# Attention and mixture-of-experts kernel: when the weights of the experts are fetched

## The chip, the cores and the metric

One core of one Trainium2 chip runs the whole program in a single launch. The metric is the time of the program on the device in microseconds (us), as the median of the runs shown. A profiled execution gives a trace: the start and the length of every instruction on the five engines (TensorE is PE, its weight loads PEld, VectorE is DVE, ScalarE is ACT, GpSimd is POOL, SyncE is SP) and of the packets that the 16 DMA engines move.

## The reference

Inputs are q, k and v of shape (8 batches, 8 heads, 576 positions, 64), a gate matrix (512 x 8), and for each of 8 experts w1 (512 x 1024) and w2 (1024 x 512), all float32, and a capacity of 80.

```python
scores = scale * np.matmul(q, k.transpose(0, 1, 3, 2))
mask = block_i >= block_j                  # causal in blocks of 64
attn = softmax(where(mask, scores, -1e9))
x = matmul(attn, v)                        # 4608 tokens x 512
logits = x @ w_gate; expert_idx = argmax(logits); gate_w = the winner's probability
for e in range(8):
    tok_idx = tokens of expert e, at most capacity (80), those with the largest gate_w
    h = np.maximum(x[tok_idx] @ w1[e], 0.0)
    out[tok_idx] = gate_w[tok_idx, None] * (h @ w2[e])
```

All rows of `out` that no expert takes are zero.

## The kernel before, in words

**Attention.** The work is cut into 32 pairs of heads (8 batches x 4 pairs), run in turns i of some 8 us. A table of steps (TURN) says what is issued in a turn, and for which pair: loads of Q and K (`ld`) for the pair five turns ahead, their transposes on DVE (`T`, line 639) two turns ahead, V (`vn`, `vt`) three turns ahead, then scores on PE (line 663), maxima on DVE, exponentials on ACT, transposes of the probabilities on PE (line 744), their copies out of PSUM (`PT`, line 792, on ACT or DVE), and the products with V (line 770). Each engine works through its own list in order. Q loads, half of the K loads and the stores go out on SP's queue; from pair 5 on the other half of the K loads, and V, go out on POOL's. Loads have four buffers each. After four pairs a batch's result goes to a scratch in DRAM (`xs`, line 429). In the last five turns SP also writes zeros over the output (18 x 512 KB).

**Weights.** There are 16 weight tiles of 2 MB, in the order w1[0], w2[0], w1[1], w2[1], and so on to w2[7]. Three of them (FW0) have memory of their own and are loaded during attention, in 16 pieces on POOL's queue: 4 of 512 KB for w1[0], 8 of 256 KB for w2[0], 4 of 512 KB for w1[1]. The generator `early` hands out one piece per `next`, in two of every three turns (line 914).

The other 13 tiles need memory that attention held, so they come at the end, on SP's queue, one DMA each (line 362). They have nine buffers in all, the three early ones included; from the tenth tile on a tile waits until its buffer's last user is through.

**Choice of tokens.** After the last pair the kernel finds, for each expert, the rows of x to take (`gi`), and gathers them from `xs` by indirect DMAs on POOL's queue (`xg`, `fetch`, line 1101): those of experts 0, 1 and 2 at once, later ones after the first product of the expert three before. DVE divides each by the sums of the softmax (`xn`, line 1211), PE transposes them (line 1254; for expert 0 line 1275), and each expert e makes `first(e)` with w1 (lines 1227 and 1240) and `second(e)` with w2 (line 1325, results in `av`, `ps`, and for the last expert `pm`); a scatter on POOL's queue writes the rows out.

**Order of the late tiles.** `half()` issues the first half (1 MB) of w2[1] while the tokens are still being chosen; the second half waits for `fetches[HOLD]`, HOLD = 1, that is for gather 1 to land. Then a list `behind` gives each tile what it waits for: w1[2] the second half's landing, w2[2] gather 1, and every later one of the first six the landing of the tile two before it.

The places that the change touches, in a few lines:

```python
if i >= 2 and i % 3:
    next(early, None)
...
other_half(fetches[HOLD])
behind = [loaded.ins, fetches[HOLD]]
for _ in range(FWA + FWC + FWB - 1):
    weights(1, behind.pop(0))
    behind.append(loaded.ins)
```

Of the kernel before, what the change touches and what calls it, by code (L numbers as in the profile page):

```python
# [7 lines left out]
F32 = mybir.dt.float32  # L8
# [10 lines left out]
P = 128  # L19
BLK = 64  # L20
NT = 5
FW0, FWA, FWC, FWB = 3, 3, 1, 2
# [166 lines left out]
def tile_attn_moe(ctx, tc, q, k, v, w_gate, w1, w2, capacity, out, xs=None, dbg=None):  # L189
# [3 lines left out]
    E, _, F = w1.shape  # L193
# [5 lines left out]
    KP = DM // P  # L199
# [55 lines left out]
    def clear(i, eng=nc.gpsimd):  # L255
        if ov is not None:
            if 0 <= i < nz:
                return eng.dma_start(ov[i], zero.rearrange("p (r d) -> p r d", r=2))
        elif i == 0:
            for j in range(NTOK // BLK):  # L260
                nc.sync.dma_start(out[j * BLK:(j + 1) * BLK, :], zero[0:BLK, 0:DM])
# [18 lines left out]
    after = const.tile([P, P], F32, name="after")  # L280
# [15 lines left out]
    def constants():  # L296
        nc.gpsimd.memset(dl, 1e-9)
        nc.gpsimd.memset(zero, 0.0)
        nc.gpsimd.iota(iota_e, pattern=[[1, E]], base=-E, channel_multiplier=0,
                       allow_small_or_imprecise_dtypes=True)  # L300
        nc.gpsimd.iota(iota_v, pattern=[[0, NT], [1, E]], base=-E, channel_multiplier=0,
                       allow_small_or_imprecise_dtypes=True)
        nc.gpsimd.memset(iota_v[0:BLK, 0], 64.0)
        nc.gpsimd.memset(lgT[:, 0:BLK], 0.0)
        nc.gpsimd.memset(sameR3, 0.0)
        nc.gpsimd.memset(ones, 1.0)
        nc.gpsimd.iota(iota_s, pattern=[[1, CHUNK]], base=0, channel_multiplier=0,
                       allow_small_or_imprecise_dtypes=True)
        nc.gpsimd.iota(iota_p, pattern=[[0, 1]], base=0, channel_multiplier=1, allow_small_or_imprecise_dtypes=True)
        nc.gpsimd.iota(iota_c, pattern=[[1, 16]], base=0, channel_multiplier=0,  # L310
                       allow_small_or_imprecise_dtypes=True)
# [14 lines left out]
    def constants3():  # L326

        nc.vector.tensor_tensor(iota_c16, sameR, iota_c, op=ALU.mult)
        nc.vector.tensor_reduce(iota_r, iota_c16, axis=AX.X, op=ALU.add)
        nc.vector.scalar_tensor_tensor(cap, cf[:, 1:2], 4294967296.0, cf[:, 0:1], op0=ALU.mult, op1=ALU.add)  # L330
        nc.vector.tensor_tensor(caplt, iota_p, cap, op=ALU.is_lt)

    nw, loaded = 0, None
    wpools = [wp] * FW0

    wlist = [x for e in range(E) for x in ((w1, e), (w2, e))]
    wt_ = {}
# [5 lines left out]
    def loads(n, after=None):  # L343

        nonlocal nw, loaded
        for _ in range(n):
            src, e = wlist[nw]
            w_ = wpools[nw % len(wpools)].tile([P, KP * F], F32, name="w")
            nw += 1
            wt_[src is w2, e] = w_ = w_.rearrange("p (a f) -> p a f", f=src.shape[2])  # L350
            if nw <= FW0:
                yield from (nc.gpsimd.dma_start(w_[:, a], src[e][a * P:(a + 1) * P]) for a in range(w_.shape[1]))
                continue
            piece(w_, src[e], 0, w_.shape[1], after)

    def piece(w_, src, a0, a1, after=None):

        nonlocal loaded
        with ExitStack() as order:
            if loaded is not None:  # L360
                order.enter_context(tc.issue_after(loaded.ins))
            loaded = nc.sync.dma_start(w_[:, a0:a1], src[a0 * P:a1 * P].rearrange("(a p) f -> p a f", p=P))
        if after is not None:
            tc.add_manual_dep(loaded.ins, after.name, mybir.DependencyInfo(
                mybir.DependencyClass.Sync, mybir.DependencyReason.DATA))

    def half():

        nonlocal nw
        src, e = wlist[nw]  # L370
        w_ = wpools[nw % len(wpools)].tile([P, KP * F], F32, name="w")
        nw += 1
        wt_[src is w2, e] = w_ = w_.rearrange("p (a f) -> p a f", f=src.shape[2])
        na = w_.shape[1]
        piece(w_, src[e], 0, na // 2)
        return lambda after: piece(w_, src[e], na // 2, na, after)

    Pt = [{u: pb.tile([P, 2, w], F32, name=f"P{u}_{i}") for u, w in WIDE.items()} for i in range(2)]  # L380

# [9 lines left out]
    def banks(use, where=BANKS):  # L391
        return [psp[i].tile([P, 512], F32, name=f"bank{i}") for i in where[use]]
# [401 lines left out]
    def warm(n, wt, after=None):  # L794

        if not n:
            return
        with ExitStack() as order:
            if after is not None:
                order.enter_context(tc.issue_after(after.ins))  # L800
            for i in range(n):
                last = nc.tensor.matmul(wt.rearrange("p (a c) -> p a c", c=P), lhsT=identr,
                                        rhs=identr.unsqueeze(1).broadcast_to([P, 4, P]), start=(i == 0),
                                        stop=(i == n - 1))
        return last
# [86 lines left out]
    with tc.manual_schedule():  # L892
        warm(WARM[0], banks("g")[0])
        early = loads(FW0)
        for i in range(-LEAD, n):
            held.clear()
            if i == -1:
                nc.sync.dma_start(ci, capacity.bitcast(U32).partition_broadcast(P))
                for h in range(2):
                    nc.sync.dma_start(wgd[h * D:(h + 1) * D, :, h * E:(h + 1) * E], wg_v[h])  # L900

            for _ in range(min(5, nz - kept - cleared) if i >= n - 5 else 0):
                clear(cleared, nc.sync)
                cleared += 1
            if i == 1 - LEAD:
                nc.scalar.activation(early_exp, ramp[:, 2, 0:1], AF.Exp)
                constants()
            if i == -1:
                constants2()
            if i == 5:  # L910
                nc.gpsimd.tensor_copy(cf, ci)
            if i == 7:
                constants3()
            if i >= 2 and i % 3:
                next(early, None)
            shared = i > 1 and (i < NP or i % NP == 0)
            for d, what, *args in FIRST if i == -1 else AHEAD if i == -2 else LAST if i == n - 1 else SHARED if shared else TURN:
                if what in slots_:
                    slots_[what]()
                elif 0 <= i + d < n and not (what == "flip" and n - NP <= i + d < n - 2):  # L920
                    getattr(pairs[i + d], what)(*args)
            if n - NP <= i + valued < n - 2:
                pairs[i + valued].flip()
            if i >= flipped and (i - flipped) % NP == NP - 1 and i - flipped < n - 1:
                enqueue(batches[(i - flipped) // NP])
        for _ in early:
            pass
        while not turns:
            t()
        bt = batches[B - 1]  # L930
        pairs[n - 2].flip()
        for _ in recips[0]:
            pass
        bt.store_sums()
        pairs[n - 1].take("V00", "a")
        bt.flip(NP - 1, 0, 8)
        pairs[n - 1].take("V01", "a")
        pairs[n - 1].take("V1", "v")
        att.close()
        fwa = late.enter_context(tc.tile_pool(name="fwa", bufs=FWA, **right, **tw))  # L940
        wpools += [fwa] * FWA
        bt.logits2(LAST_BANKS)
        bt.logits_by_token(NP - 1)
        bt_, mark = turns.pop(0)
        bt_.turn2(banks("av")[0])
        mark()
        for _ in bt.products(range(NP - 1)):
            pass
        bt.flip(NP - 1, 8, S // 32)
        bt.store_x()  # L950
        other_half = half()
        for _ in (*bt.products((NP - 1,)), *bt.shift()):
            pass
        bt.expo()
        nc.gpsimd.tensor_copy(seen[0:1], dl[0:1, 0, 0:1])
        found, weighed = bt.first_of(), bt.weight()
        for g_ in (found, found, found, weighed, found, weighed):
            next(g_)
        bt.turn_gated()
        bt.turn2(banks("L")[0])  # L960
        while small:
            t()
        for _ in bt.placed():
            pass
# [52 lines left out]
        for h in range(2):  # L1017
            vec.max_index(cidx[:, h], cand16[:, h], Wf[:, h * HW:(h + 1) * HW])

    HOLD = 1  # L1020
    pen = sel.tile([P, 2, NH], F32, name="pen")
    pool.tensor_scalar(pen, key, scalar1=0.0, scalar2=8192.0, op0=ALU.is_lt, op1=ALU.mult)
    pool.tensor_tensor(pen, pen, iota_c[:, 0:NH].unsqueeze(1).broadcast_to([P, 2, NH]), op=ALU.add)
# [71 lines left out]
    xg, fetches = [], []  # L1095
# [100 lines left out]
    wpools += [fwc] * FWC + [fwb] * FWB  # L1196

    assert cleared == nz or ov is None
    other_half(fetches[HOLD])
    behind = [loaded.ins, fetches[HOLD]]  # L1200
    for _ in range(FWA + FWC + FWB - 1):
        weights(1, behind.pop(0))
        behind.append(loaded.ins)

# [369 lines left out]
```

## Time and profile before

| what | value |
|---|---|
| runs | 385.63, 386.33, 386.37 us; median 386.33 |
| profiled execution | 387.1 us, of which the trace's span is 385.3 |
| mean granted TensorE clock | 0.997 of full speed |
| PE busy in the span | 367.5 us (95%) |
| ACT, DVE, POOL busy | 287.5, 286.0, 183.7 us |
| read from HBM, written to it | 63.21 MB, 20.33 MB |
| weight pieces on POOL's queue | 8 of 512 KB, 8 of 256 KB |
| late weight tiles on SP's queue | 12 of 2048 KB, 2 halves of 1024 KB |

Attention takes the time up to about 277 us, the choice of the tokens up to about 293, the eight experts the rest. Busy PE is not PE at its peak, and a share of the DMA engines above 1 means that packets of one engine overlap. Idle time of an engine that nothing waits for costs nothing; so the first question of any row is who waits behind it.

### The profile page before, as it was taken

To read this page: it belongs to the slowest core of one execution; us is meant where nothing else is said; L and a number is where in the kernel's file an instruction comes from. 1 tells how busy PE (TensorE), PEld (TensorE's weight loads), DVE (VectorE), ACT (ScalarE), POOL (GpSimd) and SP (SyncE) were. 2 spreads that over 40 slices of the span, in tenths; PEclk is the share of its full clock that TensorE was granted. 3 is DMA by queue.
4 is the path that set the end of the run, shared out by engine and by line. 5 is a ranking of instruction groups with operands and counts; after the bars stand their busy time and mean duration, and the time that the engine had idled before them with its cause. 6 is when DMAs were issued, how large, how long until landed. Compare 5 with 4: busy or idle time off the path is not lost. (4 is left out here: it accounts for less than half of the span.)

```text
span 385.3 us, 15173 instructions
## 1 busy us (share of the span) xinstructions
PE 367.5 (95%) x5973; PEld 248.4 (64%) x5973; DVE 286.0 (74%) x804; ACT 287.5 (75%) x880; POOL 183.7 (48%) x377
## 2 busy tenths in 40 slices
PE   5899899999999999999999999999999999999983
PEld 3566567666766666676676676666668555555652
DVE  5889799999999999999999999999986210101001
ACT  1799799999999999999999999999521333332221
POOL 6246376665976766786587664430132121110000
PEclk9999999999999999999999999999999999999998
DMA  9969999999999999999999999999795899999950
GB/s 125 154 120 187 133 184 173 154 231 132 164 215 151 162 202 181 155 176 196 177 174 245 145 182 191 279 393 407 157 212 167 278 384 374 384 391 398 399 211 26
DMA packets 169937, 84.43 MB, mean 219 GB/s; under 512 B 132590, under 2 KB 151886, under 8 KB 169857
## 3 DMA queue, kind: packets, MB, share of 16 engines
q1 hardware_dynamic: 158368, 61.80, 76.3%
q0 software_dynamic: 9120, 21.27, 24.2%
q8 instruction: 49, 0.80, 1.0%
q10 hardware_dynamic: 2368, 0.30, 0.6%
q14 instruction: 32, 0.25, 0.3%
HBM read 63.21 MB, written 20.33 MB: 217 GB/s over the span
## 5 line engine op out<-in xcount | busy, mean ns | idle before, releaser
L710 ACT ACTIVATE P<-bank,negm 128x512 f32<-128x512 f32 (+3 forms) x320 | 157.6, 549 | 10.6 <-DVE negm L699 5.9
L663 PE MATMUL bank<-T,qt 64*128 64x320 f32 (+3 forms) x512 | 98.8, 494 | 1.4 <-DVE PT L792 1.3
L770 PE MATMUL bank<-PT,vn 128*64 128x64 f32 (+3 forms) x1288 | 88.9, 292 | 0.0
L699 DVE TENSOR_REDUCE negm<-bank 128x1 f32<-128x320 f32 (+2 forms) x192 | 83.4, 474 | 5.6 <-PE bank L689 5.4
L792 ACT COPY PT<-bank 128x512 f32<-128x512 f32 x149 | 77.2, 636 | 3.8 <-PE bank L744 3.3
L770 PEld LDWEIGHTS bank<-PT,vn 128*64 128x64 f32 x1288 | 57.1, 137 | 26.7 <-ACT PT L792 3.4
L646 POOL TENSOR_SCALAR qt<-T 128x128 f32<-128x128 f32 (+2 forms) x96 | 31.2, 344 | 88.4 <-DVE T L639 88.4
L744 PEld LDWEIGHTS bank<-ident,P 64*128 64x128 f32 (+1 forms) x1600 | 58.0, 137 | 11.8 <-issue 6.6
L663 PEld LDWEIGHTS bank<-T,qt 64*128 64x128 f32 x512 | 47.9, 187 | 26.8 <-ACT PT L792 15.2
L744 PE MATMUL bank<-ident,P 64*128 64x64 f32 (+1 forms) x1600 | 63.5, 225 | 1.3 <-ACT P L710 0.6
L710 ACT ACTIVATION_READ_ACCUMULATOR P<-bank,negm 128x1 f32 x256 | 61.7, 241 | 0.0
L699 DVE TENSOR_REDUCE raw<-bank 128x1 f32<-128x64 f32 (+1 forms) x128 | 51.8, 444 | 2.3 <-PE bank L663 2.0
L639 DVE STREAM_TRANSPOSE T<-ld 128x576 f32<-128x576 f32 x64 | 49.1, 768 | 5.7 <-DMA ld<-in_k_dram 4.0
L632 POOL DMA_DIRECT2D vn<-in_v_dram x58 | 45.8, 792 | 1.2 <-issue 0.7
L1325 PE MATMUL av<-w,hT 128*32 128x512 f32 (+2 forms) x320 | 39.0, 553 | 0.0
L624 POOL DMA_DIRECT2D ld<-in_k_dram x54 | 37.3, 695 | 2.7 <-DMA ld<-in_q_dram 2.7
L1334 DVE SCALAR_TENSOR_TENSOR y<-av,comb,yt 80x512 f32<-80x512 f32 (+1 forms) x8 | 5.6, 696 | 43.0 <-ACT yt L1332 42.9
L1240 PE MATMUL ps<-xsT,w 128*64 128x80 f32 x896 | 33.1, 234 | 0.3 <-issue 0.3
L1240 PEld LDWEIGHTS ps<-xsT,w 128*64 128x64 f32 x896 | 31.9, 137 | 1.9 <-PE av L1325 1.0
L1340 POOL DMA_INDIRECT out_dram<-y,si x8 | 7.5, 936 | 53.6 <-DVE y L1334 41.3
L1332 ACT ACTIVATE yt<-ps,gfar 32x512 f32<-32x512 f32 (+2 forms) x18 | 11.4, 635 | 26.1 <-PE ps L1325 26.0
L792 DVE COPY PT<-bank 128x512 f32<-128x512 f32 x43 | 29.3, 683 | 0.3
(202 smaller groups left out, 423.9 us busy)
## 6 DMA issues: line engine op xcount, KB each, us to landing
w<-in_moe_w_dram SPq DMA_DIRECT2D x12, 2048.0 KB, 17.6
xs<-Y SPq DMA_DIRECT2D x32, 288.0 KB, 5.5
out_dram<-zero SPq DMA_DIRECT2D x18, 512.0 KB, 7.6
ld<-in_q_dram SPq DMA_DIRECT2D x126, 72.0 KB, 5.5
vn<-in_v_dram POOLq DMA_DIRECT2D x58, 128.0 KB, 5.1
ld<-in_k_dram SPq DMA_DIRECT2D x72, 72.0 KB, 5.3
w<-in_moe_w_dram POOLq DMA_DIRECT2D x8, 512.0 KB, 6.6
ld<-in_k_dram POOLq DMA_DIRECT2D x54, 72.0 KB, 6.4
```

Of the source, the lines that this page charges most:

```text
L624: eng.dma_start(self.nat[x][r], (q, k)[x][b, h0 + h, :, 32 * i:32 * i + 32] .rearrange("(g r) d -> r g d", r=32))
L632: eng.dma_start(self.vn[:, h], v[b, h0 + h, 0:512].rearrange("(j p) d -> p j d", p=P))
L639: nc.vector.transpose(t, self.nat[x].rearrange("p g d -> p (g d)"))
L646: nc.gpsimd.tensor_scalar(qb[:, to], tb[:, of], scalar1=SCALE, scalar2=1.0, op0=ALU.mult, op1=ALU.mult)
L663: nc.tensor.matmul(s[h][:, c:c + n], lhsT=q_[:, P * t - BLK:P * t + BLK], rhs=k_[:, 0:n], start=(c == 0 and g != "2"), stop=(g == "1"))
L699: nc.vector.tensor_reduce(to[:, b, h:h + 1], self.s[g][h][:, c:c + n], axis=AX.X, op=ALU.max, negate=True)
L710: nc.scalar.activation(Pt[self.i % 2][u][:, h, c1:c1 + n], self.s[g][h][:, c:c + n], AF.Exp, bias=self.negm[:, t, h:h + 1], scale=1.0, acc ...
L744: nc.tensor.transpose(pt[c][0:cols.stop - cols.start, n_ * BLK:(n_ + 1) * BLK], row[u][r, h, cols], ident[r, r])
L770: nc.tensor.matmul(a4[r] if c0 is None else av[r, BLK * c0:BLK * (c0 + b1 - b0)], lhsT=self.vn[:, h, j, :], rhs=self.PT[:, h, row, b0:b1]. ...
L792: (nc.scalar.copy if (eng or TAKE[x]) == "a" else nc.vector.tensor_copy)(*self.out.pop(x))
L1240: last = nc.tensor.matmul(dst(b)[64 * c:64 * (c + 1)], lhsT=w_[:, a, col:col + 64], rhs=x_[a], start=(a == 0), stop=(a == n - 1))
L1325: last = nc.tensor.matmul(to[col:col + s1 - s0, c0:c1], lhsT=hT[:, a, s0:s1], rhs=w_[:, a, c0:c1], start=(a == ends[0]), stop=(a == ends[1 ...
```

## The change

Three edits. The early pieces are handed out from turn 6 on, in place of turn 2. `half()` is gone: w2[1] is one DMA like the others. HOLD is 0, and w2[1] and w1[2] both wait for gather 0; w2[2] then waits for w2[1], w1[3] for w1[2], and so on.

```diff
-    def half():
-        nonlocal nw
-        src, e = wlist[nw]
-        w_ = wpools[nw % len(wpools)].tile([P, KP * F], F32, name="w")
-        nw += 1
-        wt_[src is w2, e] = w_ = w_.rearrange("p (a f) -> p a f", f=src.shape[2])
-        na = w_.shape[1]
-        piece(w_, src[e], 0, na // 2)
-        return lambda after: piece(w_, src[e], na // 2, na, after)
...
-            if i >= 2 and i % 3:
+            if i >= 6 and i % 3:
                 next(early, None)
...
-        other_half = half()
...
-    HOLD = 1
+    HOLD = 0
...
-    other_half(fetches[HOLD])
-    behind = [loaded.ins, fetches[HOLD]]
-    for _ in range(FWA + FWC + FWB - 1):
+    behind = [fetches[HOLD], fetches[HOLD]]
+    for _ in range(FWA + FWC + FWB):
         weights(1, behind.pop(0))
         behind.append(loaded.ins)
```

POOL's list around the start of turn 2, before the change (`w` is a weight piece, `vn` and `vt` V, `ld` K, `qt` the scaled Q):

```order
L646 TENSOR_SCALAR qt_145<-T_653 128x384
L632 DMA vn<-in_v_dram 128x4x64 x2
L634 DMA vt_146<-in_v_dram 64x2x64
L352 DMA w<-in_moe_w_dram 128x1024
L624 DMA ld_674<-in_k_dram 32x18x32 x2
L646 TENSOR_SCALAR qt_144<-T_814 128x128
```

and after it (the lines of the file are 13 lower):

```order
L633 TENSOR_SCALAR qt_145<-T_653 128x384
L619 DMA vn<-in_v_dram 128x4x64 x2
L621 DMA vt_146<-in_v_dram 64x2x64
L611 DMA ld_672<-in_k_dram 32x18x32 x2
L633 TENSOR_SCALAR qt_144<-T_812 128x128
```

The piece between `vt` and the K loads is gone there. The 16 pieces now stand at turns 7, 8, 10, 11 (w1[0]), 13, 14, 16, 17, 19, 20, 22, 23 (w2[0]) and 25, 26, 28, 29 (w1[1]); before they stood at 2, 4, 5, 7, then 8 to 19, then 20, 22, 23, 25. The last of them comes after the last V load on POOL's queue.

SP's list where the late tiles begin, before, with the semaphores that each waits for (DMAHW and DMASW are the landings of DMAs of SP's and of POOL's queue; DMASW5, 6 and 7 are gathers 0, 1 and 2):

```order
L429 DMA xs<-Y 32x18x128 [waits DMAHW7_49]
L362 DMA w<-in_moe_w_dram 128x4x512 [waits DMASW4_49,DMASW3_49,DMASW5_49,DMASW2_49,DMASW6_49,DMASW1_49,DMASW7_49,DMASW0_49,DMAHW0_49,PE_49,Activation_49]
L362 DMA w<-in_moe_w_dram 128x4x512 [waits DMAHW1_49,DMASW6_49]
L362 DMA w<-in_moe_w_dram 128x4x1024 [waits DMASW4_49,DMASW1_49,DMAHW1_49,PE_49,DMAHW2_49,Activation_49,Pool_49]
L362 DMA w<-in_moe_w_dram 128x8x512 [waits DMAHW3_49]
L362 DMA w<-in_moe_w_dram 128x4x1024 [waits DMAHW4_49,DMAHW2_49]
```

and after:

```order
L416 DMA xs<-Y 32x18x128 [waits DMAHW7_49]
L362 DMA w<-in_moe_w_dram 128x8x512 [waits DMASW4_49,DMASW3_49,DMASW5_49,DMASW2_49,DMASW6_49,DMASW1_49,DMASW7_49,DMASW0_49,DMAHW0_49,PE_49,Activation_49]
L362 DMA w<-in_moe_w_dram 128x4x1024 [waits DMASW4_49,DMASW3_49,DMASW7_49,PE_49,DMAHW1_49,Activation_49,Pool_49]
L362 DMA w<-in_moe_w_dram 128x8x512 [waits DMAHW2_49,DMAHW0_49]
L362 DMA w<-in_moe_w_dram 128x4x1024 [waits DMAHW3_49,DMAHW1_49]
```

The two half DMAs (128x4x512) are one (128x8x512). Before, the third row waited for the second half (DMAHW1) as well as for its own lane (DMAHW2); now the second row waits for no other weight, and the third for the first (DMAHW0). The waits for DMASW4, 3 and 7 in the second row are those for V loads whose memory the tile takes (before DMASW4 and 1).

DVE's list after the first gathers, before (`xn` is the division of a gather; the first row here is gather 1's, the later one gather 2's):

```order
L1211 TENSOR_TENSOR xn<-xg 80x128 x4
L1148 COPY gfar<-comb 32x8 x2
L1148 COPY gfar<-comb 16x8
L1155 CAST ids<-gi 80x8
L1161 TENSOR_SCALAR vm,nval<-cand 128x12
L1163 TENSOR_TENSOR chk<-slot,cap 128x2
L1171 MEMSET dif 128x8
L1211 TENSOR_TENSOR xn<-xg 80x128 x4
L1190 TENSOR_SCALAR comb<-ids 80x8
```

and after, from the same `dif` on:

```order
L1157 MEMSET dif 128x8
L1176 TENSOR_SCALAR comb<-ids 80x8
L1148 TENSOR_SCALAR chk<-sameE,nval 128x8
L1154 TENSOR_SCALAR good<-pm,iota_p,caplt 80x8
L1164 TENSOR_REDUCE nb<-pm 128x1
L1158 SCALAR_TENSOR_TENSOR dif<-occ,caplt,good 80x8
L1160 TENSOR_REDUCE dsum<-dif 128x1
L1162 SCALAR_TENSOR_TENSOR dsb<-cap,dsum 128x1
L1196 TENSOR_TENSOR xn<-xg 80x128 x4
```

Gather 2's division has moved behind the checks that end in `dsb`. PE's and ACT's lists are the same as before.

## Rows read from the trace of the kernel before

**Rows 1.** Waits of PE, whole span: us in total, times, longest

```profile
PE pm L1325 <- SPq L1386: 1.7, 1, 1.7
PE bank L663 <- DVE PT L792: 1.3, 1, 1.3
```

**Rows 2.** Timeline of PE, 370.5 to 374: start, length, what, idle before

```profile
373.38 0.52 PE L1325 MATMUL pm<-w,hT 128*32 128x384 f32 x3 [1.73 <-SPq L1386]
```

**Rows 3.** Timeline of SP's queue, the issues of late weight tiles

```profile
293.28 0.39 SPq L362 DMA_DIRECT2D w<-in_moe_w_dram  x1
...
299.33 0.37 SPq L362 DMA_DIRECT2D w<-in_moe_w_dram  x1
...
347.83 7.43 SPq L362 DMA_DIRECT2D w<-in_moe_w_dram  x1
```

**Rows 4.** DMA issues at 299.33 and 347.83: count, KB, us to landing

```profile
w<-in_moe_w_dram SPq DMA_DIRECT2D x1, 2048.0 KB, 8.5
...
w<-in_moe_w_dram SPq DMA_DIRECT2D x1, 2048.0 KB, 25.4
```

**Rows 5.** Stretches: engines' busy us, clock, DMA share, GB/s

```profile
298.00:300.00 2.00, 2.00 (x42) 1.25 (x42) 0.00 (x0) 0.44 (x1) 0.71 (x1) 1.00 0.06 18
...
302.00:371.00 69.00, 68.65 (x1220) 42.38 (x1214) 10.31 (x33) 22.56 (x40) 10.46 (x11) 1.00 1.03 386
```

**Rows 6.** Timeline of all engines, 28 to 46

```profile
31.95 0.59 POOL L352 DMA_DIRECT2D w<-in_moe_w_dram  x1
...
32.05 1.09 SPq L624 DMA_DIRECT2D ld<-in_k_dram  x2
...
35.82 2.40 PEld L770 LDWEIGHTS bank<-PT,vn 128*64 128x64 f32 x38 [0.54 <-DMA vn<-in_v_dram]
...
39.01 0.27 PE L776 MATMUL bank<-PT,vt 64*64 64x64 f32 x1 [0.19 <-DMA vt<-in_v_dram]
...
41.42 0.78 DVE L639 STREAM_TRANSPOSE T<-ld 128x576 f32<-128x576 f32 x1 [2.78 <-DMA ld<-in_k_dram]
...
43.36 1.99 PE L663 MATMUL bank<-T,qt 64*128 64x512 f32 x12 [1.28 <-DVE PT L792]
```

**Rows 7.** The stretch 35 to 40, columns as in rows 5

```profile
35.00:40.00 5.00, 4.81 (x64) 3.25 (x62) 3.61 (x9) 4.87 (x19) 3.17 (x7) 1.00 1.24 177
```

**Rows 8.** Waits of DVE from 30 to 260, the only one for a load

```profile
DVE T L639 <- DMA ld<-in_k_dram: 2.8, 1, 2.8
```

**Rows 9.** The pieces' line: count, ns min/median/max, first and last start

```profile
L352 POOL DMA_DIRECT2D w<-in_moe_w_dram x16: 568/574/591, 32.0 to 220.7; - x16
```

**Rows 10.** The stretch 276 to 278, columns as in rows 5

```profile
276.00:278.00 2.00, 1.74 (x55) 1.46 (x52) 1.68 (x8) 0.37 (x1) 0.33 (x2) 1.00 0.18 21
```

**Rows 11.** The last store of x (issued 280.23): KB, us to landing

```profile
xs<-Y SPq DMA_DIRECT2D x1, 288.0 KB, 5.2
```

**Rows 12.** Timeline of POOL, 288 to 301: the gathers of experts 0 to 3

```profile
288.71 1.13 POOL L1101 DMA_INDIRECT xg<-xs,gi  x1 [3.46 <-DVE gp L1115]
290.14 0.99 POOL L1101 DMA_INDIRECT xg<-xs,gi  x1 [0.30 <-issue]
291.43 0.97 POOL L1101 DMA_INDIRECT xg<-xs,gi  x1 [0.31 <-issue]
299.29 0.96 POOL L1101 DMA_INDIRECT xg<-xs,gi  x1 [6.88 <-PE ps L1240]
```

**Rows 13.** Timeline of DVE, 290.5 to 300: divisions of gathers 0 and 1

```profile
291.94 0.89 DVE L1211 TENSOR_TENSOR xn<-xg 80x128 f32<-80x128 f32 x4 [0.50 <-DMA xg<-xs,gi]
293.29 0.90 DVE L1211 TENSOR_TENSOR xn<-xg 80x128 f32<-80x128 f32 x4 [0.45 <-DMA xg<-xs,gi]
```

**Rows 14.** DMA issues at 291.43 and 299.29: us to landing

```profile
xg<-xs,gi POOLq DMA_INDIRECT x1, 3.0
...
xg<-xs,gi POOLq DMA_INDIRECT x1, 6.9
```

**Rows 15.** Timeline of PE, 293 to 305: transposes of expert 1's input

```profile
296.27 0.50 PE L1254 MATMUL pm<-ident,xn 80*128 80x80 f32 x4
```

## The prediction, made before the changed kernel was run

> **What bounds the kernel now.** Read first who TensorE (PE) waited for over the whole span [rows 1]. Apart from the 4.2 us at the start there are two waits over a microsecond: 1.7 us before `pm` of line 1325, the second product of the last expert, and 1.3 us before `bank` of line 663, a score matmul early in the attention part. PE is busy through nearly everything else, so time can be gained only at places where PE stands still, and lost where a new wait arises.
>
> The timeline puts the first wait at the very end: PE resumes at 373.38 after 1.73 idle, so it was free at 371.65 [rows 2]. The view names SyncE's line 1386 as releaser, but that branch was long done. The other candidate is a DMA: the last weight tile was issued at 347.83 and took 25.4 us, so it landed at 373.2 [rows 3, 4], 0.15 before PE moved. The last weight tile sets the end. Its stream runs at 386 GB/s with the DMA engines fully taken from 302 to 371, but from 298 to 300 they moved only 18 GB/s [rows 5]: a hole. It comes from the code: after the first half of tile w2[1] (1 MB, issued ahead of the gathers), the other half waits for the second gather (issued 293.28), and the next tile waits for that half (issued 299.33) [rows 3].
>
> The early wait is a chain. VectorE (DVE) idles 2.78 us before a transpose of K at 41.42, for the K loads; PE idles 0.19 at 39.01 for a V load and 1.28 at 43.36 for what DVE produced after that transpose. The K loads that land late were issued by SyncE at 32.05, right behind the first early weight piece, which GpSimd issued at 31.95 [rows 6].
>
> **The change part by part.**
>
> *Early pieces from turn 6.* The 16 pieces stay the same; the one at 31.95, and those of turns 4 and 5, go five turns or more later. What stood behind the piece was its 512 KB. At the 177 GB/s that all queues moved from 35 to 40 [rows 7] this is 524 KB / 177 = 2.96 us; at the 386 GB/s of [rows 5] it is 1.36 us. The K loads, which released DVE at about 41.3, land 1.36 to 2.96 earlier; DVE's 2.78 shrink by as much as there is. PE's 1.28 at 43.36 needs 1.28 of that, so it goes at both ends, and the V load's 0.19 with it: 1.28 + 0.19 = 1.47. More is possible: the PE weight load at 35.82 waited 0.54 for another V load [rows 6], part of which may go, so up to 2.0. Less is possible too, if what follows is not ready sooner; the lower end is 0. I take 1.5, at the row's own two gaps, because nothing else of PE stands in the way: its 50 transposes before 43.36 had ended 1.28 earlier. A turn saved here moves everything after it, since from 50 to 260 DVE never waits for a K or Q load again [rows 8] and PE waits for next to nothing [rows 1].
>
> On this the Trainium skill ("DMA: Bandwidth & Descriptors", section "Anatomy of one DMA — SWDGE (gpsimd) path") gives a fit of 2.0 us plus bytes / 436 GB/s; by that the piece occupies the engines 1.2 us, and as an estimate only 1.2 of the 1.28 would go, a sum of 1.4. The trace moved much less than 436 GB/s in that stretch [rows 7], so I stay with the row.
>
> What the pieces cost where they now stand: the four 512 KB pieces of w1[0] at turns 7, 8, 10 and 11 (three of these held 256 KB pieces), and two 512 KB pieces more at turns 28 and 29. The other 15 pieces of before, seven of them of 512 KB and the last at 220.7 [rows 9], are followed by no DVE wait for a load [rows 8]: their cover is the five turns that loads run ahead. Cost 0. At turns 28 and 29 the zeroing of the output already fills the DMA engines; 1 MB more is 1.05 MB / 386 = 2.7 us of backlog. The row 276 to 278 shows a share of 0.18, so 1.6 us of it vanish there [rows 10]; the remaining 1.1 would delay the last stores of x, which landed at 280.23 + 5.2 = 285.4 [rows 11]. The first gather started at 288.71, held by its indices [rows 12], 3.3 us later. Cost 0; without that cover 1.1.
>
> *No half tile, everything behind the first gather.* Three edits, one answer. Gather 0 is in use at 291.94 and gather 1 at 293.29 [rows 13], and SyncE issued its half at 293.28. So the release moves from 293.28 to about 291.93. In the changed order the first two whole tiles, w2[1] and w1[2], are both released there, and the third waits for the first of them: two are always in flight, and the hole at 298 to 300 has no cause left. The pair that before went out at 299.33 (w1[2] and w2[2]) was in the same state: two whole tiles into idle queues. From there on before and after have the same chain, with 7.40 us lead (299.33 - 291.93) and one tile more to move. One tile costs (373.2 - 307.8) / 11 = 5.95 us, from the landing of w1[2] (299.33 + 8.5) to that of the last tile [rows 3, 4], other traffic included. So the last tile lands 7.40 - 5.95 = 1.45 earlier, at 371.8. PE is free at 371.65 and resumes 0.15 after the landing: 371.95 in place of 373.38, a gain of 1.43. Bounds: at the pure rate a tile costs 2.097 MB / 386 = 5.43, the lead is 1.97 and the whole 1.73 goes; with gather 2's 166 KB (0.43 us) now inside the stream on top of 6.4 for a slow tile, the lead is 0.6. I take 1.43. What is late next is PE itself: behind the last product nothing changes.
>
> The cost of this edit is on the gathers. Gather 1 (issued 290.14) now has weights released 1.8 us behind it. Before, gather 2 (291.43) had a half tile released 1.85 us behind it and took 3.0 us to land; gather 3 at 299.29, with two tiles released at its side, took 6.9 [rows 12, 14]. Gather 1 stands as gather 2 did: about 3, as now. Gather 2 will take up to 6.9, landing at 298.3; its division in DVE moves behind the checks in the new order, and PE wants it only for the third expert's input, after 304. Cost 0.
>
> **The sum.** Profiled execution: 387.1 (span 385.3). 387.1 - 1.5 - 1.43 = 384.2. The median of the three runs is 386.33, 0.8 below it: 386.33 - 2.9 = 383.4.
>
> **The rivals.**
>
> A. *Only the tail gains.* The shift of turn 3 is swallowed later, by a DMA backlog that stands anyway (the share is above 1 from 35 to 40 [rows 7]). Against it: the quiet of DVE afterwards [rows 8]. 386.33 - 1.43 = 384.9.
>
> B. *The missing half is missed.* It is 1 MB that travelled while the engines were partly idle. If the hole stays (some other wait holds the second tile), the last tile lands 1.05 MB / 386 = 2.7 later, less 1.35 for the earlier release: 374.6, PE 1.35 later than before; with the early gain 386.33 - 1.5 + 1.35 = 386.2, no change. The Trainium skill ("Perfetto Trace Analysis", section "DMA Optimizations") speaks for this side: splitting a DMA lets part of it start sooner when the engines are idle. Before does show the half going ahead, and also the hole right behind the split tile [rows 5].
>
> C. *Gather 1 is caught behind the weights.* If it takes 6.9, it lands at 297.0; 0.9 us of divisions [rows 13] bring 297.9 against PE's transposes at 296.27 [rows 15]: PE stalls 1.7. That eats the wait at the end, no more: the tail gains nothing, 386.33 - 1.5 = 384.8.
>
> D. *The pieces cost the same wherever they stand: slower.* Each 512 KB piece at turns 7, 8, 10 and 11 brings PE the 1.47 that the one of turn 2 brought: 4 x 1.47 = 5.9 against 2.9 gained, 386.33 + 3.0 = 389.3. It decides where K loads are issued under some 9 us before DVE needs them, as at 32.05 for 41.42; from two collisions on the gain is gone. Against it: the pieces at 50 to 221 collided with nothing visible [rows 8, 9].
>
> E. *The change doesn't do what it says*: the release still waits for gather 1 through another semaphore, and turn 3 waits for loads late anyway. 386.3.
>
> **How the numbers follow.** Forecast 0.67, A 0.10, B 0.08, C 0.07, D 0.06, E 0.02. About 0.2% (0.8 us) is what a measurement of this kernel can tell from no change. Faster: forecast, A and C, 0.84. Same: B and E, rounded to 0.09. Slower: D and a piece of B without the early gain, 0.07. The forecast's own range is 386.33 - 2.0 - 1.73 = 382.6 to 386.33 - 1.3 - 0.6 = 384.4; for 8 in 10 it reaches over A and C, to 385.2, and down to 382.4.
>
> **What would show it.** In the changed profile: no DVE wait for K near 41 and no PE wait of 1.28 near 43; every event of the tail some 1.5 earlier; two whole tiles issued within a microsecond of each other just after gather 0; no stretch under 100 GB/s between the first tile and the last; PE's wait before the last `pm` under 0.5 us; gather 2 slower, gather 1 as before. Wrong would be: a DVE wait for loads at turns 8 to 12, or a PE wait before the transposes of the second expert's input.

## The result, and the profile after

Six runs of each kernel, side by side: before 386.87 us median (385.63 to 388.76), after 382.91 (382.71 to 383.15). The ratio is 0.9892, with an interval of 0.9864 to 0.992. All ratios of this document leave out runs that lie over 1.5% above the fastest of their kernel, nine of twelve in e11 and three in e3, so that those two are read by their medians. The forecast was 383.4 (382.4 to 385.2), faster: right. The profiled execution took 382.95 (span 381.2), against 387.1 (span 385.3).

The gain came out larger than worked out, 3.96 against 2.93, and one thing stands beside it that the forecast did not have: the kernel before scatters over three microseconds, the one after over half a microsecond. Most of the experiments are about this.

Waits of PE in the changed kernel, the largest after the 4.2 us at the start (us in total, times, longest). Line numbers are 13 to 15 lower than before:

```profile
PE bank L731 <- ACT P L697: 0.6, 1, 0.6
PE pm L1310 <- ACT hT L1280: 0.6, 1, 0.6
PE bank L566 <- DVE sp L555: 0.5, 1, 0.5
```

The 1.7 of the last product is 0.6, and the 1.3 of turn 3 is gone [rows 1]. Turn 2 in the timeline, without the piece that stood at 31.95 [rows 6]:

```profile
31.98 1.09 SPq L611 DMA_DIRECT2D ld<-in_k_dram  x2
...
35.51 2.75 PE L757 MATMUL bank<-PT,vn 128*64 128x320 f32 x40
38.19 0.27 PE L762 MATMUL bank<-PT,vn 64*64 64x64 f32 x1
...
39.00 0.73 DVE L626 STREAM_TRANSPOSE T<-ld 128x576 f32<-128x576 f32 x1
```

DVE transposes this K at 39.00 with no wait, where before it waited 2.78 and started at 41.42. Also, the 40 products with V take 2.75. The same row of the kernel before:

```profile
35.08 3.48 PE L770 MATMUL bank<-PT,vn 128*64 128x320 f32 x40
```

Take the start of each PE instruction before minus after, and call it the lead. It is -0.43 just before 35 us (the start differs a little from run to run), 0.80 at 39, 2.24 at 44, 2.3 from 50 to 140 and 2.7 from 150 to 298. So turns 2 and 3 gave 2.7: 1.2 up to 39, where V was late, and 1.4 from there to 44, where K was. The further 0.3 came near 145; its cause is not shown.

The gathers and the stream of weights, after. GpSimd's timeline and SyncE's queue, then the DMA issues of 288 to 292, that at 288.74 and that at 296.60 (count, KB, us to landing), then two stretches (columns as in rows 5):

```profile
286.01 1.14 POOL L1087 DMA_INDIRECT xg<-xs,gi  x1 [3.44 <-DVE gp L1101]
...
296.60 0.96 POOL L1087 DMA_INDIRECT xg<-xs,gi  x1 [6.90 <-PE ps L1225]
```

```profile
289.43 10.22 SPq L362 DMA_DIRECT2D w<-in_moe_w_dram  x3
```

```profile
w<-in_moe_w_dram SPq DMA_DIRECT2D x2, 2048.0 KB, 12.5
...
xg<-xs,gi POOLq DMA_INDIRECT x1, 4.0
...
xg<-xs,gi POOLq DMA_INDIRECT x1, 7.4
```

```profile
298.00:300.00 2.00, 2.00 (x24) 0.60 (x20) 0.00 (x0) 0.00 (x0) 0.00 (x0) 1.00 1.03 411
302.00:367.00 65.00, 65.00 (x1167) 40.21 (x1164) 10.26 (x33) 21.26 (x39) 10.54 (x11) 1.00 1.03 385
```

Where 18 GB/s moved at 298 to 300 [rows 5], 411 do. Two tiles go out at 289.43 and 290.05, right behind gather 0. The lead of 2.7 at 298 falls to 1.8 at 305, is back at 2.7 at 352, and is 4.0 from the last product to the end: the tail gave 1.3. The last product, PE and ACT:

```profile
368.87 0.44 ACT L1280 ACTIVATE hT<-ps 128x320 f32<-128x320 f32 x1 [1.78 <-PE ps L1225]
369.38 0.52 PE L1310 MATMUL pm<-w,hT 128*32 128x384 f32 x3 [0.56 <-ACT hT L1280]
```

The view puts the 0.56 down to ACT, but the last tile landed at 369.25 too, 0.13 ahead of PE. Which of the two it is stays open up to the last experiment.

### The profile page after: what moved, and what is told of

Its sections match the earlier page's. It is cut to its first block, busy times and chain, and to the rows that moved or that the text cites. A ratio compares the mean times of both kernels' runs of the same rounds, so it can differ in the third digit from the quotient of the medians.

```text
span 381.2 us, 15172 instructions
## 1 busy us (share of the span) xinstructions
PE 366.9 (96%) x5973; PEld 247.1 (65%) x5973; DVE 286.1 (75%) x804; ACT 286.8 (75%) x880; POOL 183.5 (48%) x377
## 4 chain that ended last, share of the span: by engine, by line
PE 86%; DVE 7%; ACT 3%; DMA 1%; issue 1%; POOL 0%; POOLq 0%; DVEq 0%; SPq 0%; ACTq 0%
PE bank L650 21%; PE bank L757 20%; PE bank L731 13%; PE av L1310 9%; PE ps L1225 9%; PE bank L425 2%; PE bank L762 2%; ACT P L697 2%; DVE raw L686 2%; DVE negm L686 1%; PE bank L667 1%; DMA xs<-Y 1%; PE ps L789 1%; PE ps L1310 1%; PE pm L1310 1%
## 5 line engine op out<-in xcount | busy, mean ns | idle before, releaser
L1310 PE MATMUL ps<-w,hT 128*32 128x512 f32 (+2 forms) x72 | 29.3, 548 | 0.3 <-issue 0.3
```

What stands on the lines that cost most here:

```text
L1310: last = nc.tensor.matmul(to[col:col + s1 - s0, c0:c1], lhsT=hT[:, a, s0:s1], rhs=w_[:, a, c0:c1], start=(a == ends[0]), stop=(a == ends[1 ...
```

## The experiments

Each kernel ran up to 12 times, beside the kernel before on the same chip. The times of the kernel before range from 383.6 to 391.8 there, and so do those of some variants. The medians are over all runs. "Low clock" counts the runs whose mean granted TensorE clock was 0.993 or less; "full clock" is 0.994 or more. This line was drawn with the runs in view, and the times on its two sides overlap: in the first group of the kernel before, 386.36 to 391.75 at low clock and 384.63 to 388.51 at full clock.

| kernel | early pieces from turn | ahead of the gathers | median (range) | low clock | ratio to before |
|---|---|---|---|---|---|
| before, three groups | 2 | half tile | 388.05, 388.33, 387.38 | 45 of 88 | 1 |
| e1_early | 6 | half | 384.98 (384.15 to 388.67) | 2 of 12 | 0.9959 [0.9931, 0.9987] |
| e2_tail | 2 | none | 384.64 (383.60 to 388.33) | 1 of 12 | 0.9946 [0.9913, 0.9978] |
| e3_turn3 | 4 | half | 388.48 (383.09 to 389.46) | 9 of 12 | 0.9982 [0.9934, 1.003] |
| e4_behind | end of 2 | half | 386.73 (383.98 to 389.74) | 6 of 12 | 0.9984 [0.9945, 1.0022] |
| e5_half_unchained | 2 | half, no chain | 387.15 (383.81 to 389.91) | 5 of 12 | 0.9962 [0.9922, 1.0002] |
| e6_half_first | 6 | half, no chain | 383.36 (382.12 to 388.07) | 1 of 6 | 0.987 [0.9823, 0.9916] |
| e7_second_gather | 6 | none | 384.09 (383.35 to 384.88) | 0 of 7 | 0.9901 [0.9865, 0.9937] |
| e8_dense | 6, every turn | none | 383.91 (383.05 to 391.2) | 2 of 12 | 0.9925 [0.989, 0.9959] |
| e9_after | 6 | none | 383.18 (382.44 to 387.87) | 1 of 12 | 0.9919 [0.9885, 0.9954] |
| e10_no_half | 2 | none | 386.7 (384.45 to 391.59) | 2 of 12 | 0.9981 [0.9944, 1.0018] |
| e11_three_quarters | 2 | three quarters | 389.85 (382.84 to 391.19) | 11 of 12 | 0.9982 [0.991, 1.0053] |
| e12_quarter_first | 6 | quarter, no chain | 382.8 (382.26 to 383.49) | 0 of 6 | 0.989 [0.9847, 0.9933] |

e1 to e4 share one group of the kernel before, e5 to e8 the second, e9 to e12 the third. The groups ran on different chips, so times of different groups are compared with care: at full clock the medians of the kernel before are 386.51, 386.21 and 385.80.

**e1_early: the first part alone.**

```
-            if i >= 2 and i % 3:
+            if i >= 6 and i % 3:
```

> Only the first part of the change: no early weight piece before turn 6; the half tile and its chain stay as before. Theory T (the two parts add up, and the early part is worth what the two traces differ by at 44 us, about 2.7): about 384.2, the lead of PE over the kernel before about 2.5 at 44 us and still there at the end, because the last weight tile is released by a gather and so moves with the selection. Rival 1 (the early part is worth what was predicted, 1.5): 385.4. Rival 2 (the last tiles end at the same time whatever attention does, so a lead of attention is lost in the tail): 386.7.

Measured 384.98, 3.1 under its group's median. By runs at full clock it is 384.83 against 386.51, a gain of 1.7. Rival 2 falls: the lead is kept. Between theory T (2.7) and rival 1 (1.5), the full-clock runs lie nearer to rival 1, but the interval of the ratio (a gain of 0.5 to 2.7) holds both.

**e2_tail: the second part alone** (the changed kernel with `i >= 2`).

```
-            if i >= 6 and i % 3:
+            if i >= 2 and i % 3:
```

> Only the second part: no half tile, every later tile behind gather 0; the early pieces start at turn 2 as before. Theory T: the tail gains the 1.3 that the two traces show behind 352 us, so about 385.6. Rival 1 (the tail's gain is the predicted 1.43 and the early part 1.5 plus noise of the profile): 385.4, not to be told from T by this run alone, only with the other half. Rival 2 (the tail alone does everything, the early lead is lost): about 383.0.

Measured 384.64; at full clock 384.58 against 386.51, a gain of 1.9, where 1.43 was predicted. Both parts pay by themselves. By medians over all runs they would add up to 6.5, but the changed kernel measured beside its own group gains 4.2 (e9). They are not independent: each alone already removes most of the low-clock runs. At full clock they add up to 3.6, against 2.7 for both together in e9's group; that these groups differ by 0.7 before any change leaves open whether the parts add up there.

**e3_turn3: one piece taken away.**

```
-            if i >= 2 and i % 3:
+            if i >= 3 and i % 3:
```

> Kernel before with turn 2's piece alone taken away (pieces at turns 4, 5, 7 and so on; the sixteenth comes one place later). Theory T: the K loads of turn 2 (asked for at 31.98 and 32.58, right behind the piece at 31.95) are what the early pieces hold up, so nearly all of the early part comes from this one piece: about 384.3, as when all pieces wait for turn 6. Rival (the pieces of turns 4 and 5 cost as much each, a third of the early part per piece): about 386.0.

A miss: 388.48, no better than before. In its trace DVE waits for no load from 30 to 52, so turn 3 is mended as expected. But behind it PE waits 3.1 us for the rows of gather 0. GpSimd, PE, the gathers' us to landing, and stretches:

```profile
286.39 1.13 POOL L1101 DMA_INDIRECT xg<-xs,gi  x1 [4.10 <-DVE gp L1122]
```

```profile
292.99 0.80 PE L1275 MATMUL pm<-ident,xn 80*128 80x80 f32 x3 [3.08 <-DVE xn L1211]
```

```profile
xg<-xs,gi POOLq DMA_INDIRECT x3, 4.7
```

```profile
284.00:290.00 6.00, 5.79 (x37) 3.91 (x36) 2.73 (x14) 0.34 (x2) 3.00 (x3) 1.00 0.82 229
290.00:294.00 4.00, 1.01 (x7) 0.83 (x9) 1.35 (x7) 0.58 (x3) 0.08 (x1) 0.81 0.29 79
294.00:298.00 4.00, 4.00 (x57) 3.69 (x57) 2.19 (x16) 0.28 (x2) 0.00 (x0) 0.50 0.75 266
298.00:302.00 4.00, 4.00 (x85) 3.59 (x86) 0.86 (x5) 0.98 (x3) 0.00 (x0) 0.84 0.51 159
```

Read the last but two column, the granted clock: behind a stretch in which PE was busy 1.01 us of 4, it stands at 0.50 (1.2 of 2.4 GHz) from 294 to 298 and is back at full after 302. The half tile went out at 281.82, as early as in the profiled run of the kernel before (281.81, the first of the two issues behind the stores). But attention ended 3.0 earlier, and gather 0 started at 286.39 and not at 288.71 [rows 12]. The half's packets move from 285 to 291, so now the gather runs among them. The gain of attention was spent on a collision, with a lower clock on top. Three of the twelve runs were at full clock: 383.1 to 385.2, as theory T had it.

**e4_behind: the piece moved to the end of turn 2.**

```
+            if i == 2:
+                next(early, None)
```

(with `i >= 3` as in e3.)

> Kernel before with turn 2's piece moved behind that turn's own issues, not taken away: the same bytes in the same turn. Theory T (order: a load that is asked for first has its packets in front): the K loads land near 37 us as in the changed kernel, and the time is about 384.3. Rival (bytes: 0.5 MB within these microseconds slows whatever else is under way): K loads still land near 40 us and the time is about 386.5.

Measured 386.73, and it does not tell order from bytes: the piece went out at 39.87 in the trace, a turn later, so no piece stood near those K loads at all. DVE waited only 0.3 for them, up to 38.83. Yet PE waited for a V load there:

```profile
37.13 2.75 PE L770 MATMUL bank<-PT,vn 128*64 128x320 f32 x38 [1.36 <-DMA vn<-in_v_dram]
```

So turn 2's V can be late without any piece. The trace also has the collision (PE waits 3.5 for gather 0). Inconclusive as a test of order.

**e5_half_unchained: the hole taken away, the half kept.**

```
-    behind = [loaded.ins, fetches[HOLD]]
+    behind = [fetches[HOLD], loaded.ins]
```

> Kernel before with one dependence changed: the first whole tile waits for gather 1 alone and not for the second half tile too, so two transfers start at once; the half tile ahead of the gathers stays, and so do the early pieces. Theory H (what the tail won came from the hole in the weights' stream at 298 to 300 us, not from leaving out the half): the hole goes, the stream runs at its 386 GB/s from 291 us on with 0.4 of a tile less behind it, so the last tile lands 3 to 5 us earlier and PE's last wait of 1.73 falls to at most the 0.56 that the changed kernel shows: about 385.7. Rival (the half itself delays the gathers and so what follows): no better than 386.7.

Measured 387.15; expected 385.7. The stream did what theory H says: with the release where it was (293.06 against 293.28), the last tile lands 26.8 behind its issue at 343.08, at 369.9 and not at 373.2. PE asks for it at 372.26 and does not wait, though PE itself is late here by the wait below. Waits of PE from 285 to 372, the largest, then the stretch of the hole, and the last tile (us to landing):

```profile
PE pm L1275 <- DVE xn L1211: 2.4, 1, 2.4
```

```profile
298.00:300.00 2.00, 2.00 (x53) 1.93 (x53) 0.86 (x5) 0.84 (x2) 0.00 (x0) 1.00 1.01 392
```

```profile
w<-in_moe_w_dram SPq DMA_DIRECT2D x1, 2048.0 KB, 26.8
```

But here too the half met the gathers. The hole explains the last wait; taking it away gains little as long as the half stands where it does (the interval of the ratio holds no change).

**e6_half_first: early pieces late, no hole, release by gather 0, half kept.** The edits of e1 and e5, and:

```
-    HOLD = 1
+    HOLD = 0
```

> Early pieces from turn 6, the half tile kept, its second half and the first whole tile both behind gather 0. The earliest stream of weights tried: the last tile should land some 3 us before PE asks for it. Theory F (PE's last wait of 0.56 in the changed kernel is for ACT's gelu output, and the weights only happen to land with it): PE still waits about 0.5, the time is that of the changed kernel, 382.9. Rival W (that wait is for the last tile): the wait is gone, about 382.3. A second rival (the half ahead of the gathers delays them more than it saves): over 383.3.

Median 383.36: five runs of 382.12 to 383.49 and one of 388.07. The last tile lands at 367.5, and PE starts the last product at 369.57 without a wait, as rival W has it. So the 0.56 of the changed kernel is no floor. (The activation there is a relu, not the gelu of the expectation.) By the time, though, the second rival (over 383.3) is nearest. In the traced run the gain was lost elsewhere: PE stood 0.96 at 298.38, with no releaser that the profile shows.

**e7_second_gather: the changed kernel, released by gather 1.**

```
-    HOLD = 0
+    HOLD = 1
```

> The changed kernel with the weights released by gather 1 instead of gather 0, still without a half tile. Gather 1 lands 1.4 us after gather 0. Theory T (weights bound the end): last tile 1.4 later, PE's last wait 0.6 grows to 2.0, about 384.3. Rival (the gathers then land undisturbed and the stream catches up): 383.0.

Measured 384.09, near theory T's 384.3; the changed kernel did not run in this group, so the waits of the trace say more than the time. The weights bound the tail, at two products now:

```profile
PE ps L1225 <- SPq L1371: 0.9, 1, 0.9
PE pm L1310 <- SPq L1371: 0.7, 1, 0.7
```

**e8_dense: a piece in every turn from 6 to 21.**

```
-            if i >= 6 and i % 3:
+            if i >= 6:
```

> The changed kernel with a piece in every turn from 6 to 21 instead of two turns in three. Theory T (only turn 2 is short of DMA time, later turns have loads far ahead): 382.9, no DVE wait for a load. Rival D (a piece that meets K and V loads costs about 1.5 wherever it stands, and now those meet that were kept apart): 384.4 or more, with DVE waits for loads in turns 6, 9 and so on.

Measured 383.91, between theory T and rival D, some 0.7 to 1 over the changed kernel's two medians (of other groups). Its trace against the changed one's loses 0.7 at 140 and 0.9 at 195 to 200. DVE waits for loads, from 30 to 260:

```profile
DVE T L626 <- DMA ld<-in_q_dram: 1.2, 2, 0.9
```

So pieces side by side do cost something, about 0.1 each. Rival D's 1.5 each is refuted.

**e9_after and e10_no_half: is the scatter the half tile's?** e9 is the changed kernel once more. e10 is the kernel before with only the half taken out (in the changed kernel, `i >= 2` and `HOLD = 1`).

> The changed kernel itself, on the same chip as the three that follow. Theory C (the scatter of the kernel before, 384 to 391 us, comes from the half tile: in the traces of three kernels with it, e3, e4 and e5, its packets were still moving when the gathers began, PE waited 2.4 to 3.5 us for the gathered rows, and the granted clock fell to 0.5 behind that wait): without a half tile the runs lie within 382.5 to 384.5, median 383.0, while the kernel before scatters beside it. Rival N (the scatter is the chip's and has nothing to do with the kernel): the changed kernel scatters here over 5 us as well.

> The kernel before with nothing but the half tile taken out: early pieces from turn 2, later tiles behind gather 1. Theory C: no wait for gathered rows in 290 to 296 us, full clock there, median about 385.5 (the changed kernel plus 1.5 for turn 2's piece and 1.1 for the later release), hardly a run over 387.5. Rival N: as many runs over 387.5 as the kernel before has.

e9: 383.18, eleven of twelve runs within 382.4 to 384.4, while 12 of 29 runs of the kernel before beside it have the low clock. That speaks for theory C. e10: 386.7, five runs over 387.5. That is what rival N says, since 13 of 29 runs of the kernel before lie there too, and against C as it was put. But of these five only two have the low clock; at full clock e10 spreads from 384.45 to 389.12. Sorted by clock, which no expectation had planned, the runs point to two sources. The half, where early pieces stand as well, brings the low clock: of the kernels with early pieces before turn 6, those with a half or more have it in 76 of 136 runs, those without in 3 of 24. The half alone is not enough: with the pieces from turn 6 (e1, e6) it is 3 of 18. The pieces of turns 2 to 5 bring a spread at full clock: the kernels without them (e1, e6 to e9, e12) have no full-clock run over 385.7. What those long full-clock runs wait for no trace shows: e10's profile fell on its fastest run, with a DVE wait for K of 1.0 and a PE wait of 0.6 in turn 3.

**e11_three_quarters: the suspected cost, larger.**

```
-        piece(w_, src[e], 0, na // 2)
-        return lambda after: piece(w_, src[e], na // 2, na, after)
+        piece(w_, src[e], 0, 3 * na // 4)
+        return lambda after: piece(w_, src[e], 3 * na // 4, na, after)
```

> The kernel before with three quarters of that tile ahead of the gathers in place of a half (1.57 MB in place of 1.05). Theory C: the packets last 1.4 us longer at the 386 GB/s of the stream, so the gathers meet them in every run; PE waits 3 to 5 us for the gathered rows, the clock falls behind it, median 389 or more. Rival N, or that the gathers pass the weights: no more than the kernel before, and some 1.5 less where the last tile comes earlier.

Measured 389.85, eleven of twelve runs with the low clock: as theory C has it. GpSimd, the us to landing, PE, and stretches:

```profile
288.80 1.13 POOL L1101 DMA_INDIRECT xg<-xs,gi  x1 [5.83 <-DMA xs<-Y]
```

```profile
xg<-xs,gi POOLq DMA_INDIRECT x3, 7.2
```

```profile
297.37 0.80 PE L1275 MATMUL pm<-ident,xn 80*128 80x80 f32 x3 [6.80 <-DVE xn L1211]
```

```profile
294.00:298.00 4.00, 0.63 (x3) 0.55 (x3) 0.98 (x5) 0.20 (x1) 0.00 (x0) 0.50 0.25 65
298.00:302.00 4.00, 4.00 (x52) 3.59 (x53) 2.57 (x18) 0.65 (x4) 0.00 (x0) 0.50 0.43 135
```

The first row shows why half and gather meet. The gather waits for the last store of x to land, and the early part of the tile is queued right behind that store. Where the store, and not the selection, is what the gather waits for last, the gather starts 0.9 us behind its landing (e5 and e11) and runs into the weights. The distance tells the cases apart: in e3, e4, e5 and e11 gather 0 starts 4.5 to 4.6 us behind the issue of the early part, and PE waits for it; in e6 it is 5.5, and in the kernel before, e1 and e12 6.8 to 6.9, and PE has no such wait.

**e12_quarter_first: a version that may beat both** (e6 with a quarter instead of a half).

```
+        piece(w_, src[e], 0, na // 4)
+        return lambda after: piece(w_, src[e], na // 4, na, after)
```

> A kernel that may beat both: early pieces from turn 6, a quarter of the tile (0.52 MB) ahead of the gathers, the rest and the next tile behind gather 0. Theory C with weights as the bound of the last wait: the quarter is through before the gathers start, the last tile lands about 1.4 us earlier than in the changed kernel, PE's last wait of 0.56 is gone: 382.4, with no scatter. Rival: what is won at the last tile is lost elsewhere (PE's idle time of 0.96 at 298 us with half a tile): 382.9 or more.

Median 382.8, all six runs within 382.26 to 383.49: the lowest median of the study, with no low clock in six runs. Against e9 in the same group it is 0.4 better (0.1%), less than can be told apart. Its last product:

```profile
368.68 0.52 PE L1325 MATMUL pm<-w,hT 128*32 128x384 f32 x3
...
368.80 0.44 ACT L1295 ACTIVATE hT<-ps 128x320 f32<-128x320 f32 x1 [1.78 <-PE ps L1240]
```

PE starts, without a wait, 0.12 before ACT begins its second `hT`. So the last product does not need that `hT` to start, and the 0.56 in the changed kernel was the last tile: the releaser that the view named there was only the event that ended nearest to PE's start. The landings agree: in seven traces (the kernel before, the changed one, e1, e7, e8, e9 and e10) PE starts the last product 0.13 to 0.14 behind the landing of the last tile.

## Why the prediction was right, step by step

*Early pieces, taken at 1.5 (0 to 2.0).* The place and the chain were right: the K wait of 2.78 and PE's 1.28 are gone, and the last of those K loads lands 5.3 behind its issue (33.09), where it took 8.2 (33.22). The profiled pair gives 2.7, over the upper bound. What was mis-sized is the V term: it was read off as 0.19, with up to 0.54 more, but the way from the V products to 39 took 3.9 before and 2.7 after, 1.2 in all. PE's listed idle time left out that its 40 products were themselves stretched (3.48 against 2.75). And e4 shows such a V wait without a piece, so part of the 2.7 belongs to that one execution.

The price was read from one execution, and that one was dear. Five traces have a piece in turn 2: the kernel before, e10, e2, e11 and e5. The last K load takes 7.0 to 8.2 in all of them, so the delay of K is shown; but DVE's wait for it is 2.8 in the kernel before [rows 8] and, in the order of the others:

```profile
DVE T L626 <- DMA ld<-in_k_dram: 1.0, 1, 1.0
DVE T L626 <- DMA ld<-in_k_dram: 0.9, 1, 0.9
DVE T L639 <- DMA ld<-in_k_dram: 0.5, 1, 0.5
DVE T L639 <- DMA ld<-in_k_dram: 0.4, 1, 0.4
```

From 34 to 50 PE loses on the changed kernel 2.7 in the first, and 0.95, 0.9, 0.45 and 0.35 in the others. That the 1.5 lies near the 1.7 of the full-clock runs (e1) is therefore partly luck: it was less than the execution lost from which it was read, and more than each of the other four lost.

*The pieces where they now stand, taken at 0.* Right: no DVE wait for a load from 30 to 260 in the changed kernel. e8 shows the limit, about 0.1 each when none is left out.

*The tail, taken at 1.43.* Right in size: 1.3 between the traces, 1.9 between full-clock runs (e2). Of its links, the hole is shown (e5: with the chain gone the last tile lands 3.4 earlier), and the earlier release too (e7: without it 384.09, and two waits for tiles). PE's last wait is 0.56, a little over the 0.5 that was named.

*The gathers, taken at 0.* Right for the changed kernel, gather 2 landing after 4.0 and not 6.9. But the step that failed as a description of the kernel before is here: the half tile was counted as 1 MB that travels while the engines are partly idle, with no cost. The profiled execution shows no cost because its selection came 3.3 us after the last store [rows 11, 12]; in about half of the other executions (45 of 88) the low clock says otherwise. No low-clock execution of the kernel before was profiled. All four profiled variants with the low clock (e3, e4, e5, e11) show the same wait for gather 0, of 2.4 to 6.8 us, and a fallen clock behind it (0.66 to 0.50); none of the other profiled runs shows either. The size fits: by its rows, e3's clock between 290 and 302 takes 0.009 off the mean of its span, and its mean is 0.986, against 0.994 or more in the full-clock runs. That every low-clock run is this collision is inferred from these four, not shown run by run. The changed kernel has no half, and with it went most of these runs: this is the third gain, which the sum did not have.

*The sum.* 2.93 predicted. At full clock and in one group, 385.80 to 383.11 is 2.7 (e9). Over all runs it is 3.96 in the first comparison and 4.2 in the third group. That the time came out within 0.5 of the 383.4 is partly luck: the three runs that the sum started from have a median 0.54 below that of the six, which makes up for half of the missing gain. The forecast's own range also took 1.3 as the low end of the early part, and not the 0 named for it.

*The rivals.* A is refuted by e1, where attention's lead lasts to the end. B: the hole is gone, and leaving the half out looks like a gain (see the gathers). The rule cited there from the Trainium skill ("Perfetto Trace Analysis", section "DMA Optimizations"), that splitting a DMA may allow part of it to start sooner, agrees with e12's quarter: the last tile lands at 367.8 against 369.25, of which 0.6 is a release that came earlier in that execution. e11 shows where it turns round. C did not occur: gather 1 landed after 3.15. D is refuted by the changed kernel itself and, but for 0.1 a piece, by e8. E is refuted by the trace: the tiles go out behind gather 0, and the waits of turn 3 are gone.

## What to carry to other kernels

A transfer sent ahead into idle DMA time is free only as long as what follows it comes late enough: when the work before it gets faster, look at what then starts among its packets. One profiled execution shows one outcome of such a race, and a price that is read from it is the price of that execution (here 2.7, where four others of the same turn lost 0.35 to 0.95). If the runs of a kernel scatter, count the granted clock of all of them, and look for the latency-bound load (here a gather that PE waits for) that sometimes falls behind bulk traffic. And a wait's size is not only the idle time in its row: compare the duration of the group that it feeds.

## What the runs showed that was not expected

- PE waits of 2.4 to 6.8 us were followed by a granted clock of 0.50 to 0.66 in the mean of the next 4 us, also while PE was fully busy again (e5, wait 2.4: 0.66 from 294 to 298; e3, wait 3.1: 0.50 there; e11, wait 6.8: 0.50 from 294 to 302, with PE busy throughout from 298). The low-clock runs of the kernel before have a median 2.8 (first group) above its full-clock ones.
- A gather of 166 KB took 3.1 on quiet engines, and 4.7 (e3) and 7.2 (e11) among the packets of a weight tile, each the median of the first three.
- Behind the release PE sometimes stood with no releaser that the profile shows, 0.96 at 298.38 in e6 (below) and 0.60 at 347.72 in e7. The one in e7 ends 0.2 behind the landing of the tile for the next product, so it may be a wait for that tile; near the one in e6 no tile landed.

```profile
298.38 0.62 PE L1325 MATMUL ps<-w,hT 128*32 128x512 f32 x1 [0.96 <-issue]
```

- Left open: the cause of these waits; why the half does less harm where the pieces begin at turn 6 (in the two traces, e1 and e6, gather 0 starts later against the half); why single runs without any half (e2, e8 to e10: 6 of 48) had the low clock; what the long full-clock runs of kernels with pieces at turns 2 to 5 waited for; and why the train of stores before the gathers ended later against the selection in e3, e4, e5 and e11 than in e1.
